# Unit 0's k through the SP queue in fp32, cast by VectorE and ScalarE, with k^T made ahead of q^T

**Chip, cores, metric.** One core of one Trainium2 chip. The metric is device time in microseconds (us) of one execution; lower is better. A run is one execution; an execution with a profile also leaves a trace.

## The reference

Two stages. Squared-ReLU attention over q, k, v of shape (8, 12, 448, 64) gives x of shape (3584, 768); two matrix products with a squared ReLU between them follow. Inputs and output are fp32.

```python
scores = scale * np.matmul(q, k.transpose(0, 1, 3, 2))
attn = np.maximum(scores, 0.0) ** 2 / S
x = np.matmul(attn, v)           # heads side by side: (3584, 768)
h = x @ w_in                     # (3584, 2048)
r = np.maximum(h, 0.0)
out = (r * r) @ w_out
```

## The kernel before

The kernel works in fp16 and fixes its own order of instructions. Attention is cut into 24 units of four heads. A unit's q and k come in as `[128, 2, 448]` tiles; for the first units TensorE transposes them by matmuls with an identity matrix that GpSimd makes (seven blocks, two halves each), and the blocks are copied out of PSUM to `qT` and `kT`. A score tile needs **one block of kT and all of qT**. Only unit 0 is exposed: nothing can hide its loads.

```python
def load16(n):
    tq = q16_p.tile([P, 2, J * D], FP16, name="q16", tag="q16")
    tk = q16_p.tile([P, 2, J * D], FP16, name="k16", tag="k16")
    nc.gpsimd.dma_start(out=tq, in_=heads(q, n))     # casts fp32 to fp16 on the way
    nc.gpsimd.dma_start(out=tk, in_=heads(k, n))
    q16s[n] = (tq, tk)

load16(0)
... # make_identity(nc, ident) on GpSimd; zeros on VectorE; a first ACTIVATE
load16(1); load_v(0); load16(2); load_v(1); load_v(2)

def turn_first(ps):
    ts = new_qkt()                                    # qT, kT
    for i, src in enumerate(q16s.pop(0)):             # q first, then k
        tps = slot(FP16)[:, i, 0:J * P].rearrange("p (j c) -> p j c", j=J)
        for j in range(J):
            for hh in range(2):
                nc.tensor.transpose(tps[64 * hh:64 * hh + 64, j],
                                    src[:, hh, j * D:(j + 1) * D], ident)
        if i:
            nc.scalar.activation(out=ts[i][:, 0], in_=tps[:, 0], func=AF.Copy)
        nc.vector.tensor_copy(ts[i][:, i:J], tps[:, i:J])
        warm(ps, 1)                                   # a matmul on zeros
    qkt[0] = ts

...
warm(ps, 10)
turn_first(ps)
s(0, 1); s(1); s(2); ...                              # scores, each evicted by ScalarE
```

A `slot` is a PSUM tile of two banks; the pool behind it holds two.

Of the kernel before, what the change touches and what calls it, by code (L numbers as in the profile page):

```python
# [11 lines left out]
FP16 = mybir.dt.float16  # L12
FP32 = mybir.dt.float32
AF = mybir.ActivationFunctionType
# [4 lines left out]
def kernel(  # L19
# [9 lines left out]
    nc = tc.nc  # L29

    B, H, S, D = q.shape
# [11 lines left out]
    P = 128  # L43
    J = 7
# [22 lines left out]
    g_p = ctx.enter_context(tc.tile_pool(name="gp", bufs=1))  # L67
    early = ExitStack()
    q16_p = early.enter_context(tc.tile_pool(name="q16p", bufs=3))

    PSUM = bass.MemoryType.PSUM
    s_p = ctx.enter_context(tc.tile_pool(name="sps", bufs=2, space=PSUM))
# [8 lines left out]
    def heads(t, n):  # L81
        b, u = divmod(n, NU)
        return t[b].rearrange(
            "(hh u hp) (p j) d -> u (hp p) hh (j d)", hh=2, hp=2, j=J)[u]
# [6 lines left out]
    def load16(n):  # L91
        tq = q16_p.tile([P, 2, J * D], FP16, name="q16", tag="q16")
        tk = q16_p.tile([P, 2, J * D], FP16, name="k16", tag="k16")
        nc.gpsimd.dma_start(out=tq, in_=heads(q, n))
        nc.gpsimd.dma_start(out=tk, in_=heads(k, n))
        q16s[n] = (tq, tk)

    def load_v(n):
        t = v_p.tile([P, 2, J * D], FP16, name="vt", tag="vt")
        nc.gpsimd.dma_start(out=t, in_=heads(v, n))  # L100
        vts[n] = t
# [12 lines left out]
    def new_qkt():  # L114
        return [qkt_p.tile([P, J, P], FP16, name=nm, tag=nm) for nm in ("qT", "kT")]
# [30 lines left out]
    def sums_w2(i):  # L146
# [4 lines left out]
        dst, x, y = ((t1, b12, b11), (t3, b22, b12), (t2, b22, t1), (nt4, b21, t2))[op]  # L151
        nc.vector.tensor_sub(dst[:, c], x[:, c], y[:, c])

    load16(0)
    ident = const_p.tile([P, P], FP16, name="ident", tag="ident")
    make_identity(nc, ident)
    zeros = const_p.tile([P, S], FP16, name="zeros", tag="zeros")
    nc.vector.memset(zeros, 0.0)
    junk = const_p.tile([P, 1], FP16, name="junk", tag="junk")
    nc.scalar.activation(out=junk, in_=zeros[:, 0:1], func=AF.Relu)  # L160
    load16(1)
    load_v(0)
    load16(2)
    load_v(1)
    load_v(2)
# [28 lines left out]
    def slot(dtype, third=False):  # L194
        return (third_p if third else s_p).tile(
            [P, 2, 2048 // mybir.dt.size(dtype)], dtype, name="slot", tag="slot")

    def warm(ps, n):
        for _ in range(n):
            nc.tensor.matmul(ps[:, 0, 0:S], lhsT=zeros[:, 0:P], rhs=zeros,  # L200
                             start=True, stop=True)

    def turn_first(ps):

        ts = new_qkt()
        for i, src in enumerate(q16s.pop(0)):
            tps = slot(FP16)[:, i, 0:J * P].rearrange("p (j c) -> p j c", j=J)
            for j in range(J):
                for hh in range(2):
                    nc.tensor.transpose(  # L210
                        tps[64 * hh:64 * hh + 64, j],
                        src[:, hh, j * D:(j + 1) * D], ident)
            if i:
                nc.scalar.activation(out=ts[i][:, 0], in_=tps[:, 0], func=AF.Copy)
            nc.vector.tensor_copy(ts[i][:, i:J], tps[:, i:J])
            warm(ps, 1)
        qkt[0] = ts

    def pe_transpose(n):
# [557 lines left out]
    ps = slot(FP32, True)  # L777
    warm(ps, 10)
    turn_first(ps)

    def s(t, times=2):
# [76 lines left out]
        name="mma", bufs=2, space=PSUM, reuse_waits="tile")))  # L858
# [5 lines left out]
    def some(part):  # L864
# [11 lines left out]
        name="mmb", bufs=2, space=PSUM, side="right", reuse_waits="tile")))  # L876
# [35 lines left out]
    for pr in range(1, B // 2):  # L912
# [3 lines left out]
        for i in range(21):  # L916
            ts = [t0 + 2 * i, t0 + 2 * i + 1]
# [86 lines left out]
```

## Time and profile before

| | before |
|---|---|
| median of 4 runs | 370.81 us (370.6 to 370.95) |
| span of the profiled run | 368.9 us |
| TensorE busy | 97% of the span |
| q landed after its issue at 1.27 us | 3.9 us |
| first score starts | 7.29 us |
| first eviction of a score by ScalarE starts | 7.72 us |

The span is the profiled execution from first to last instruction, and is about 1.8 us under the time. The lines are shown in the prediction, with a sentence on how to read each. Two habits help. In the chain of waits every piece was released by the one above it, so the sum from the top to "ACT at L266" is the length of the prologue. And the bracket at the end of a timeline line tells how long the engine idled before and which instruction or DMA ended that.

### The profile page before, as it was taken

The page shows a single profiled execution, that of the slowest core. Times are in us where ns is not written, and L with a number is a line of the kernel's source. Part 1 is how long each engine was busy: PE and PEld are TensorE (multiplying, and loading weights), DVE is VectorE, ACT ScalarE, POOL GpSimd, SP SyncE. Part 2 cuts the span into 40 slices and gives each one's busy share as a digit, 9 for nine tenths or more (in the row PEclk, how much of TensorE's full clock was granted, in tenths as well). Part 3 has the DMA queues.
Part 4 walks back from the last instruction along what each step waited for, and adds up shares of the span by engine and source line. Part 5 has one row for each costly group of instructions (what it writes and reads, how often), then busy time and mean ns, then how long its engine had stood idle before and what let it go on. Part 6 is the DMA issues. An engine that isn't in the chain of part 4 may idle for free.

```text
span 368.9 us, 8720 instructions
## 1 busy us (share of the span) xinstructions
PE 359.6 (97%) x3588; PEld 230.3 (62%) x3588; DVE 265.4 (72%) x470; ACT 247.5 (67%) x371; POOL 107.1 (29%) x128
## 2 busy tenths in 40 slices
PE   8899999999999999999999999999999999999994
PEld 3644445445555778875555588786555689976663
DVE  2997677997777787788585766989766686884442
ACT  3988894787676989876556588886765885532220
POOL 8545521846553155531225045140000000000001
PEclk9999999999999999999999999999999999999999
DMA  8999999999999999967699899692323300003333
GB/s 115 191 207 203 205 204 162 161 158 165 190 166 127 184 101 98 115 93 62 140 166 105 159 155 86 88 116 37 65 71 88 85 3 2 2 0 85 87 92 81
DMA packets 121159, 42.64 MB, mean 116 GB/s; under 512 B 100832, under 2 KB 117760, under 8 KB 121120
## 3 DMA queue, kind: packets, MB, share of 16 engines
q0 software_dynamic: 82912, 23.01, 62.3%
q1 hardware_dynamic: 38048, 18.98, 25.7%
q8 instruction: 28, 0.46, 0.5%
q10 hardware_dynamic: 160, 0.10, 0.1%
q14 instruction: 11, 0.09, 0.1%
HBM read 45.61 MB, written 11.01 MB: 153 GB/s over the span
## 4 chain that ended last, share of the span: by engine, by line
PE 90%; ACT 3%; DVE 3%; issue 2%; DMA 1%; POOL 0%; POOLq 0%; ACTq 0%
PE mm L725 34%; PE mm L538 27%; PE slot L262 10%; PE mm L409 9%; PE slot L317 7%; ACT at L266 3%; DMA k<-in_k_dram 1%; DVE at L297 1%; PE avt L280 1%; PE slot L238 1%; PE mm L238 0%; DVE at L369 0%; DVE xt L292 0%; ACT u L627 0%; DVE osb L632 0%
## 5 line engine op out<-in xcount | busy, mean ns | idle before, releaser
L266 ACT ACTIVATE at<-slot 128x896 f16<-128x896 f32 x168 | 145.8, 925 | 22.2 <-PE slot L262 22.2
L369 DVE TENSOR_TENSOR at<-at 128x896 f16<-128x896 f16 x147 | 87.1, 617 | 9.7 <-ACT at L266 9.6
L109 POOL DMA_DIRECT2D qs<-in_q_dram x36 | 35.3, 983 | 113.7 <-DMA qT<-qs 106.2
L725 PEld LDWEIGHTS <-s 128*128 128x128 f16 x440 | 41.5, 98 | 32.7 <-issue 3.6
L262 PE MATMUL slot<-qT,kT 64*64 64x448 f16 x744 | 56.8, 361 | 1.9 <-ACT at L266 1.4
L538 PEld LDWEIGHTS <-w 128*128 128x128 f16 x576 | 54.3, 98 | 5.1 <-issue 4.3
L538 PE MATMUL mm<-xt,w 128*128 128x224 f16 x432 | 48.9, 259 | 0.0
L725 PEld LDWEIGHTS <-g 128*128 128x128 f16 x336 | 31.7, 98 | 24.1 <-issue 4.7
L538 PEld LDWEIGHTS <-ws 128*128 128x128 f16 x432 | 40.3, 98 | 4.7 <-issue 4.7
L632 DVE SCALAR_TENSOR_TENSOR osb<-mm,u 128x384 f32<-128x384 f32 (+1 forms) x30 | 16.2, 542 | 36.4 <-ACT u L627 24.0
L725 PE MATMUL mm<-b,g 128*128 128x384 f16 x224 | 40.7, 326 | 0.0
L725 PE MATMUL mm<-b,s 128*128 128x384 f16 x216 | 39.6, 326 | 0.2 <-DVE s L594 0.2
L409 PE MATMUL mm<-xt,w 128*128 128x448 f16 x192 | 39.8, 354 | 0.0
L725 PE MATMUL mm<-t,s 128*128 128x384 f16 x224 | 39.3, 326 | 0.0
L109 POOL DMA_DIRECT2D ks<-in_k_dram x36 | 35.1, 976 | 9.4 <-DMA b<-in_moe_w_out_dram 5.8
L262 PEld LDWEIGHTS <-kT 64*64 64x64 f16 x744 | 19.0, 104 | 28.7 <-issue 23.3
L561 POOL DMA_DIRECT2D out_dram<-osb x2 | 1.1, 563 | 119.6 <-DVE osb L632 119.6
L627 ACT ACTIVATE u<-mm 128x384 f32<-128x384 f32 x28 | 13.8, 492 | 31.6 <-PE mm L725 27.1
L538 PE MATMUL mm<-x,ws 128*128 128x224 f16 x288 | 34.1, 259 | 0.0
L481 DVE CUSTOM_DVE_ANT_0 g<-mm,m 128x448 f16<-128x448 f32 x36 | 22.4, 622 | 15.1 <-PE mm L538 7.3
L317 PE MATMUL slot<-at,vt 64*64 64x448 f16 x588 | 31.9, 350 | 0.2 <-DVE at L369 0.2
L409 PEld LDWEIGHTS <-w 128*128 128x128 f16 x192 | 17.1, 98 | 19.2 <-issue 5.1
(76 smaller groups left out, 399.7 us busy)
## 6 DMA issues: line engine op xcount, KB each, us to landing
out_dram<-osb SPq DMA_DIRECT2D x52, 192.0 KB, 3.0
vt<-in_v_dram POOLq DMA_DIRECT2D x24, 224.0 KB, 6.2
qs<-in_q_dram POOLq DMA_DIRECT2D x36, 112.0 KB, 4.6
ks<-in_k_dram POOLq DMA_DIRECT2D x36, 112.0 KB, 5.0
w<-in_moe_w_in_dram POOLq DMA_DIRECT2D x8, 384.0 KB, 11.9
b<-in_moe_w_out_dram POOLq DMA_DIRECT2D x4, 768.0 KB, 17.1
q<-in_q_dram POOLq DMA_DIRECT2D x6, 224.0 KB, 7.9
k<-in_k_dram POOLq DMA_DIRECT2D x6, 224.0 KB, 8.3
```

What stands on the lines that cost most here:

```text
L109: nc.gpsimd.dma_start(out=t[:, :, hh, :], in_=heads(src, n)[:, hh].rearrange("p (j d) -> p j d", d=D))
L238: nc.tensor.transpose(pss[i][64 * hh:64 * hh + 64, i if n < 4 else 0, j * P:(j + 1) * P], src[:, hh, j * D:(j + 1) * D], ident)
L262: nc.tensor.matmul(ps[c, hh, 0:S], lhsT=kT[r, j, c], rhs=qT[r, :, c], start=True, stop=True)
L266: nc.scalar.activation(out=at, in_=ps[:, :, 0:S], func=AF.Relu, scale=SK)
L317: nc.tensor.matmul(ps[64 * hh:64 * hh + 64, hp, 0:S], lhsT=vt[r, hh, j * D:(j + 1) * D], rhs=at[r, hh, :], start=(j == 0), stop=(j == J - 1))
L369: lambda: nc.vector.tensor_mul(at, at, at), 0))
L409: nc.tensor.matmul(cell[0][:, 0:S], lhsT=w1[f // 4][:, m, (f % 4) * P:(f % 4 + 1) * P], rhs=xts[b][:, m, :], start=(m == 0), stop=(m == NM ...
L481: nc.vector._custom_dve(TENSOR_ADD_SAT, out=gs(s, hi, right), in0=acc(s, y), in1=keep[s, nm], s0=3.4e38, s1=0.0)
L538: nc.tensor.matmul(XY[s][y][:, r * Q:(r + 1) * Q], lhsT=left(k, i0 + 2 * s + r, m), rhs=right(k, m), start=(fresh and r == 0 and m == 0), ...
L627: nc.scalar.activation(out=t, in_=X[0][:, 0:HALF], func=AF.Copy, scale=CO)
L632: nc.vector.scalar_tensor_tensor(out=osb[row][:, c], in0=acc[0][:, 0:cc.stop - cc.start], scalar=CO, in1=keep[nm][:, cc], op0=ALU.mult, op ...
L725: nc.tensor.matmul(acc[0][:, 0:HALF], lhsT=left()[:, f], rhs=right[:, f], start=(fresh and f == 0), stop=(f == KH - 1), skip_group_check=n ...
```

## The change

Its intent: k of unit 0 doesn't queue behind q. SP starts it earlier, in fp32 (that SP could not have cast it on the way is not shown by a run; in the kernel before every load that casts is in GpSimd's queue); two idle engines cast it; k^T is then ready before q lands, and q^T is copied by two engines at once.

```diff
+        if n == 0:
+            raw = raw_p.tile([P, 2, J * D], FP32, name="rk", tag="rk")
+            nc.sync.dma_start(out=raw, in_=heads(k, n))
         nc.gpsimd.dma_start(out=tq, in_=heads(q, n))
+        if n == 0:
+            return lambda: (nc.vector.tensor_copy(tk[:, 0], raw[:, 0]),
+                            nc.scalar.activation(out=tk[:, 1], in_=raw[:, 1], func=AF.Copy))
         nc.gpsimd.dma_start(out=tk, in_=heads(k, n))
 ... # the casts are issued after the first ACTIVATE
-        for i, src in enumerate(q16s.pop(0)):
+        for i in (1, 0):
 ... # the same transposes, into tps[i]
+            warm(ps, 1)
             if i:
-                nc.scalar.activation(out=ts[i][:, 0], in_=tps[:, 0], func=AF.Copy)
-            nc.vector.tensor_copy(ts[i][:, i:J], tps[:, i:J])
-            warm(ps, 1)
+                nc.scalar.activation(out=ts[1][:, 0], in_=tps[1][:, 0], func=AF.Copy)
+        nc.vector.tensor_copy(ts[0][:, 0:4], tps[0][:, 0:4])
+        nc.scalar.activation(out=ts[0][:, 4:J], in_=tps[0][:, 4:J], func=AF.Copy)
+        nc.vector.tensor_copy(ts[1][:, 1:J], tps[1][:, 1:J])
```

More of the change, by code (lines that the diff above doesn't have):

```diff
@@ L69 @@
     q16_p = early.enter_context(tc.tile_pool(name="q16p", bufs=3))
+    raw_p = early.enter_context(tc.tile_pool(name="rawp", bufs=1))
     PSUM = bass.MemoryType.PSUM
@@ L93, in load16 @@
         tk = q16_p.tile([P, 2, J * D], FP16, name="k16", tag="k16")
+        q16s[n] = (tq, tk)
+        if n == 0:
+            raw = raw_p.tile([P, 2, J * D], FP32, name="rk", tag="rk")
+            nc.sync.dma_start(out=raw, in_=heads(k, n))
         nc.gpsimd.dma_start(out=tq, in_=heads(q, n))
+        if n == 0:
+            return lambda: (nc.vector.tensor_copy(tk[:, 0], raw[:, 0]),
+                            nc.scalar.activation(out=tk[:, 1], in_=raw[:, 1], func=AF.Copy))
         nc.gpsimd.dma_start(out=tk, in_=heads(k, n))
-        q16s[n] = (tq, tk)
     def load_v(n):
@@ L152, in sums_w2 @@
         nc.vector.tensor_sub(dst[:, c], x[:, c], y[:, c])
-    load16(0)
+    cast_k0 = load16(0)
     ident = const_p.tile([P, P], FP16, name="ident", tag="ident")
@@ L160 @@
     nc.scalar.activation(out=junk, in_=zeros[:, 0:1], func=AF.Relu)
+    cast_k0()
     load16(1)
@@ L205, in turn_first @@
         ts = new_qkt()
-        for i, src in enumerate(q16s.pop(0)):
-            tps = slot(FP16)[:, i, 0:J * P].rearrange("p (j c) -> p j c", j=J)
+        tps = {}
+        for i in (1, 0):
+            src = q16s[0][i]
+            tps[i] = slot(FP16)[:, i, 0:J * P].rearrange("p (j c) -> p j c", j=J)
             for j in range(J):
@@ L210, in turn_first @@
                     nc.tensor.transpose(
-                        tps[64 * hh:64 * hh + 64, j],
+                        tps[i][64 * hh:64 * hh + 64, j],
                         src[:, hh, j * D:(j + 1) * D], ident)
+            warm(ps, 1)
             if i:
-                nc.scalar.activation(out=ts[i][:, 0], in_=tps[:, 0], func=AF.Copy)
-            nc.vector.tensor_copy(ts[i][:, i:J], tps[:, i:J])
-            warm(ps, 1)
+                nc.scalar.activation(out=ts[1][:, 0], in_=tps[1][:, 0], func=AF.Copy)
+        nc.vector.tensor_copy(ts[0][:, 0:4], tps[0][:, 0:4])
+        nc.scalar.activation(out=ts[0][:, 4:J], in_=tps[0][:, 4:J], func=AF.Copy)
+        nc.vector.tensor_copy(ts[1][:, 1:J], tps[1][:, 1:J])
+        del q16s[0]
         qkt[0] = ts
```

## The prediction

> **What bounds the kernel now.** I read the page first (who is busy over the whole span), then the chain of waits over the first 60 us, then the timeline of the first 8 us, then the list of waits with a DMA as releaser. From the page:
>
> ```profile
> PE 359.6 (97%) x3588; PEld 230.3 (62%) x3588; DVE 265.4 (72%) x470; ACT 247.5 (67%) x371; POOL 107.1 (29%) x128
> ...
> PE 90%; ACT 3%; DVE 3%; issue 2%; DMA 1%; POOL 0%; POOLq 0%; ACTq 0%
> ```
>
> TensorE carries the kernel, and 90% of the chain that ended last is TensorE. DMA holds 1% of it, one piece: the load of k that this change touches. No gain can be larger than that piece and its neighbours. The chain of waits, first pieces (start, length, what):
>
> ```profile
> 2.12 4.17 DMA k<-in_k_dram
> 6.29 0.04 issue
> 6.33 0.60 PE slot L210 x14
> 6.94 0.02 issue
> 6.96 0.29 ACT kT L214
> 7.25 0.04 issue
> 7.29 0.41 PE slot L262 x4
> 7.70 0.02 issue
> 7.72 3.35 ACT at L266 x4
> ```
>
> This is the prologue: k lands at 6.29, is transposed, its first block is copied by ScalarE, the first score runs at 7.29, and at 7.72 the first ScalarE eviction of a score begins. From there evictions follow back to back (timeline: 6.58 us for 8, 0.82 us each), so the figure that the change must move is **7.72**. If the first eviction starts d earlier, the engine-bound chain after it starts d earlier. The timeline of the same stretch (start, length, engine, line):
>
> ```profile
> 1.16 3.92 PE L200 MATMUL slot<-zeros 128*128 128x448 f16 x10 [1.16 <-DVE zeros L158]
> 1.27 0.85 POOL L94 DMA_DIRECT2D q<-in_q_dram  x1 [0.83 <-POOLq L988]
> ...
> 2.12 0.75 POOL L95 DMA_DIRECT2D k<-in_k_dram  x1
> ...
> 5.21 0.52 PEld L210 LDWEIGHTS <-q 128*64 128x64 f16 x14 [0.93 <-DMA q<-in_q_dram]
> ...
> 5.94 0.62 DVE L215 COPY qT<-slot 128x896 f16<-128x896 f16 x1 [4.84 <-PE slot L210]
> ...
> 6.96 0.28 ACT L214 ACTIVATE kT<-slot 128x128 f16<-128x128 f16 x1 [4.72 <-PE slot L210]
> ...
> 7.27 0.56 DVE L215 COPY kT<-slot 128x768 f16<-128x768 f16 x1 [0.70 <-ACT kT L214]
> ```
>
> Three things are to be seen. q's transposes already wait for q (5.21) and k's come 1.1 us later. The ten warm-up matmuls fill TensorE until about 4.9: weight loads come every 0.373 us, the last matmul starts near 4.5. And the VectorE copy of k^T did not run beside ScalarE's copy of the same tile: the list says that it waited for it (7.24, then 7.27). Two engines that write parts of one tile are serialised here.
>
> The list of waits shows that after k no compute engine waits for an input load. All other DMA releases before the end are of the queues themselves, such as
>
> ```profile
> PEld L210 <- DMA q<-in_q_dram: 0.9, 1, 0.9
> POOL w L135 <- DMA q<-in_q_dram: 0.8, 2, 0.4
> PEld L210 <- DMA k<-in_k_dram: 0.4, 1, 0.4
> ```
>
> so earlier loads by themselves buy nothing beyond the first score.
>
> [...]
>
> **The change part by part.**
>
> 1. *k by SP.* It removes one POOL issue (0.75 us) and 4.17 us from issue to landing. SP is free at 0.7 us. Its stores of 192 KB land 2.1 us (least) to 2.8 us (median) after issue. k in fp32 is 448 KB; the loads stream some 200 GB/s as fp16 written, which is 400 GB/s as fp32 read, so 448 KB take about 1.15 us, against 0.5 us for 192 KB. Estimate: landing at 0.75 + 2.1..2.8 + 0.65 = 3.5..4.2 us.
>
> 2. *The casts.* [...]ScalarE half 0.54 us (the 128x448 row), side by side: k in fp16 is ready at 4.1..4.8. The table load ends at 2.03, so both engines are idle then.
>
> 3. *k's transposes first.* They start when the warm-ups end, S = 4.88, if the cast is in time; that is 1.45 us earlier than 6.33. At the warm clock the 14 weight loads take 0.51 us. If the clock rises near 5.4, as the slow first loads at 5.21 hint, nine of them run at 0.055 and five at 0.036: 0.70. Then one warm-up, 0.19, then q's transposes, 0.60 to their end (the chain's figure). q landed at about 5.2 before, so it isn't what they wait for. All transposes are done at 4.88 + 0.51..0.70 + 0.19 + 0.60 = 6.18..6.37, against 6.94 before: 0.57 to 0.76 us earlier. This is the gain.
>
> 4. *What follows the last transpose.* Before: ScalarE's one block of k^T, 0.29. After: all of q^T is needed by every score. The diff splits its copy, VectorE four blocks and ScalarE three, as if in parallel. The built program says otherwise: ScalarE's q^T copy waits for the third tick of VectorE's semaphore, and the ticks are memset, cast and VectorE's q^T copy. So they run one after the other, as the two k^T copies do in the trace. VectorE for 512 elements: 0.556 at 768 and 0.62 at 896 are 0.5 ns per element, so 0.43. ScalarE for 384: 278 ns + 256 x 0.825 ns = 0.49. With 0.03 between them the copies take 0.95 in place of 0.29: **0.65 us given back**. VectorE's k^T copy (0.56) runs beside ScalarE's part and is done about when the first score is, so it adds nothing.
>
> 5. *Sum.* -0.57..-0.76 + 0.65 = from 0.10 faster to 0.08 slower: first score at 7.2..7.4 (7.29 before), first eviction at 7.6..7.8 (7.72 before). After that nothing changes. POOL's later loads start some 0.7 us earlier, with k's bytes out of their queue, and nobody waited for those. The total stays: about **370.9 us**.
>
> **The rivals.**
>
> - *The copies overlap after all* (the intent of the diff). Then the first score comes 0.49 + 0.06 after the transposes, at 6.75..6.95, and the kernel gains 0.35 to 0.55 us: 370.4 to 370.6. For it: the diff is written so. Against it: the semaphore in the built program, and the same pair of engines serialised at 7.24 to 7.27.
> - *k comes late.* If SP's first load lands at 5 us instead of 4, because 256 rows of 1792 bytes are slower than my stores suggest or because it collides with q's load, then cast and transposes start near 5.6, and the first eviction at 8.4: 0.5 to 0.7 us slower, 371.5. For it: no plain load by SP is in this trace. Against it: the DMA engines show no work before 2.6 us.
> - *q comes late.* k's fp32 writes share the engines with q from 2.6 us on. q may be 0.4 us later than before (5.2) without harm, since it is not asked for before 5.6; and q no longer shares with k's other load. I give this little weight.
> - *Later loads matter.* v of unit 0 landed near 11.3 (a POOL issue that waited for it went at 11.31) and its first matmul starts at 11.50, so compute moved earlier by over 0.2 us could run into it. But POOL's queue is shorter by one load of 1.15 us, so it moves more than compute does.
>
> **Range and chances.** All outcomes lie within 1 us of 371, while 2% is 7.4 us. The spread of the three runs before is 0.35 us. Middle 370.9; low end 370.3 (copies overlap, or an early clock), high end 371.4 (k late). Faster by over 2%: 0.004. Slower by over 2%: 0.006. Within 2%: 0.99.
>
> **What the profile after should show.** Right if: k's transposes start near 4.9 with no idle TensorE between the tenth warm-up and them (step 3); [...]ScalarE's 128x384 q^T copy begins just as VectorE's 128x512 copy ends, with VectorE named as its releaser (step 4); first score within 0.15 us of 7.29; the rest of the trace shifted by that same amount. Step 1 is wrong if k's transposes name a cast or a DMA as releaser well after 5; step 4 is wrong if the two q^T copies overlap. The prediction as a whole fails if the time moves by over 0.6 us, above all if it does so with the first eviction still near 7.7: then something after the prologue depends on the loads, which I say it doesn't.

Cut from it are a paragraph of rules and figures that no trace of this case shows, and the two places that rested on them: VectorE's time for its half of the cast, and the mark that the casts end before 4.9. That time was not a term of the sum, which stands as recorded: -0.57 to -0.76 plus 0.65 us, from 0.10 faster to 0.08 slower, about 370.9 us. k's readiness at 4.1 to 4.8 rests on SP's landing at 3.5 to 4.2 and ScalarE's 0.54 us alone; that VectorE's half is the shorter no trace had shown then. SP's landing is an estimate: the measured 2.1 to 2.8 us of its 192 KB stores, and 448 KB at twice the 200 GB/s at which the trace shows the loads written in fp16. The trace before shows where the other terms come from: ScalarE's copies took 278 ns for 128 elements, 543 for 448 and 912 for 896 (0.825 ns per element from the first to the last), and 54 matmuls of 448 columns took 10.32 us (0.19 for one warm-up). The 0.055 us of a slow weight load is an estimate: in that trace the first six of q's weight loads start within 0.22 us from 5.21, and the clock record is full from 5.47.

## The result

The changed kernel takes **371.31 us** (median of 4 runs, 370.98 to 371.63) against 370.81. The ratio is 1.0014, with a 95% interval of 0.9996 to 1.0031: the same within 2%, and not clearly apart from 1. A ratio here is the mean time of one kernel's fast runs over that of the other's of the same rounds, so it isn't quite the ratio of the medians. The span grew from 368.9 to 369.2 us. The profiled run of the changed kernel was the fastest of its four (370.98), so its trace shows less of the loss than the medians do.

The chain of waits of the changed kernel, first pieces (start, length, what):

```profile
1.28 4.73 DMA q<-in_q_dram
6.00 0.04 issue
6.05 0.60 PE slot L220 x14
6.65 0.02 issue
6.67 0.44 DVE qT L226
7.11 0.02 issue
7.13 0.50 ACT qT L227
7.63 0.04 issue
7.67 0.41 PE slot L275 x4
8.08 0.02 issue
8.10 3.35 ACT at L279 x4
```

k is gone from the chain, and q has taken its place. The last transposes end at 6.65 in place of 6.94, but two copies follow one another before the first score starts at 7.67 (7.29 before). The first eviction starts at 8.10: 0.38 us later. The timeline of the same stretch:

```profile
4.25 0.58 ACT L102 ACTIVATE k<-rk 128x448 f16<-128x448 f32 x1 [2.02 <-DMA rk<-in_k_dram]
4.25 0.39 DVE L101 CAST k<-rk 128x448 f16<-128x448 f32 x1 [3.15 <-DMA rk<-in_k_dram]
4.73 0.56 PEld L220 LDWEIGHTS <-k 128*64 128x64 f16 x14 [0.46 <-DVE k L101]
...
6.04 0.42 PEld L220 LDWEIGHTS <-q 128*64 128x64 f16 x14 [0.56 <-DMA q<-in_q_dram]
6.05 0.58 PE L220 MATMUL slot<-ident,q 128*64 128x128 f16 x14 [0.29 <-DMA q<-in_q_dram]
...
7.13 0.49 ACT L227 ACTIVATE qT<-slot 128x384 f16<-128x384 f16 x1 [1.35 <-DVE qT L226]
```

k's part works as meant: cast by 4.83, transposed from 4.73 on. q's transposes then **wait for q**, whose load got slower: the weight loads for 0.56 us, the matmuls, which still had the warm-up to run, for 0.29. The list of DMA issues in the first 1.4 us (what, queue, size, us from issue to landing), of the kernel before and then of the changed one:

```profile
q<-in_q_dram POOLq DMA_DIRECT2D x1, 224.0 KB, 3.9
```

```profile
rk<-in_k_dram SPq DMA_DIRECT2D x1, 448.0 KB, 3.5
q<-in_q_dram POOLq DMA_DIRECT2D x1, 224.0 KB, 4.7
```

So there are two questions: what did the serial copies cost, and why did q land 0.8 us later?

### The profile page after: what moved, and what is told of

Its sections match the earlier page's. It is cut to its first block, busy times and chain, and to the rows that moved or that the text cites. A ratio compares the mean times of both kernels' runs of the same rounds, so it can differ in the third digit from the quotient of the medians.

```text
span 369.2 us, 8724 instructions
## 1 busy us (share of the span) xinstructions
PE 359.2 (97%) x3588; PEld 230.5 (62%) x3588; DVE 265.5 (72%) x471; ACT 248.8 (67%) x373; POOL 105.6 (29%) x127
## 4 chain that ended last, share of the span: by engine, by line
PE 90%; ACT 3%; DVE 3%; issue 1%; DMA 1%; POOL 0%; POOLq 0%; ACTq 0%
PE mm L738 34%; PE mm L551 27%; PE slot L275 10%; PE mm L422 9%; PE slot L330 7%; ACT at L279 3%; DMA q<-in_q_dram 1%; DVE at L310 1%; PE avt L293 1%; PE slot L251 1%; PE mm L251 0%; DVE at L382 0%; DVE xt L305 0%; ACT u L640 0%; DVE osb L645 0%
```

## The experiments

Twelve kernels ran. Each is told by q's landing (us after its issue), the start of the first eviction, and the span of the profiled run, beside the time. "A" edits start from the changed kernel, "B" edits from the kernel before. Single runs have no interval, and every kernel, the one before too, was traced in one execution alone: a landing or a first eviction below is that of one execution.

**One copy of q^T (A).** VectorE copies all seven blocks.

```diff
-        nc.vector.tensor_copy(ts[0][:, 0:4], tps[0][:, 0:4])
-        nc.scalar.activation(out=ts[0][:, 4:J], in_=tps[0][:, 4:J], func=AF.Copy)
+        nc.vector.tensor_copy(ts[0], tps[0])
```

> The changed kernel with q^T copied whole by VectorE, in one instruction, in place of four blocks on VectorE and then three on ScalarE. Theory (the two copies of one slot run one after the other, 0.44 + 0.02 + 0.50 = 0.96 us by the chain of waits): one copy of 896 elements takes 0.62, so the first score starts 0.33 us earlier, at 7.33, and the first eviction at 7.77 in place of 8.10; the time falls by 0.3 us to about 371.0. Rival (the copies are not what the first score waits for, q's late landing alone is): no change, first eviction at 8.10.

Measured: 371.03 us against 370.85 (ratio 1.0002, 0.9987 to 1.0017). q landed 4.8 us after issue. From the last transpose (6.75) to the first score (7.54) 0.79 us passed, where the changed kernel needed 1.02 (6.65 to 7.67). First eviction 7.97. So one engine is 0.23 us faster than two in turn. The expected 0.33 was not reached: after the single copy 0.14 us pass until the score, against 0.04 in the changed kernel.

**Two slots (A).** The last three blocks of q are transposed first and into the free bank of k's slot, so ScalarE and VectorE read different slots.

```diff
-            for j in range(J):
+            for j in ((4, 5, 6, 0, 1, 2, 3) if i == 0 else range(J)):
 ... # blocks 4 to 6 of q go to tps[2], which is bank 0 of k's slot
-        nc.scalar.activation(out=ts[0][:, 4:J], in_=tps[0][:, 4:J], func=AF.Copy)
+        nc.scalar.activation(out=ts[0][:, 4:J], in_=tps[2][:, 4:J], func=AF.Copy)
```

> The changed kernel with the last three blocks of q transposed first and into the other slot, so that ScalarE's copy shares no slot with VectorE's. Theory (the serialisation comes from sharing the slot in PSUM that is read, not from the tile that is written): ScalarE's q^T copy starts near 6.4, before VectorE's at 6.67, which ends at 7.1; first score at 7.15, first eviction at 7.58, 0.5 us before the changed kernel and 0.14 before the kernel before; time about 370.8. Rival (writing one tile from two engines serialises, or the two reads of PSUM slow each other): the copies still follow each other or take over 0.6 us each, first eviction at 8.0 or later.

Timeline of this kernel:

```profile
6.24 0.49 ACT L231 ACTIVATE qT<-slot 128x384 f16<-128x384 f16 x1 [0.54 <-PE slot L224]
...
6.46 0.42 DVE L230 COPY qT<-slot 128x512 f16<-128x512 f16 x1 [1.89 <-PE slot L224]
```

The copies now overlap, both released by TensorE, each as long as before, although both write the same `qT` tile. What serialised them was the **slot that they read**, not the tile that they write. (The wait is a semaphore in the built program, as the prediction found; no run here shows whether the hardware would need it.) From the last transpose (6.44) to the first score (7.04) 0.60 us pass in place of 1.02, so taking the serialisation away gave 0.42. q landed 4.5 us after issue, and the first eviction came at 7.46, before that of the kernel before. The profiled run had a span of 368.6 us, the shortest of all. Yet the four times were 370.38, 371.25, 371.43 and 370.26 (ratio 1.0, 0.9981 to 1.002): no gain that holds over runs. The trace is of the 370.38 run, so its early first eviction stands for the two shorter executions at most; the spans of the other two, 369.5 and 369.7, are about 1 us longer.

**Extra load (B).** The kernel before, with SP's fp32 load into a tile that nobody reads.

```diff
+        if n == 0:
+            raw = raw_p.tile([P, 2, J * D], FP32, name="rk", tag="rk")
+            nc.sync.dma_start(out=raw, in_=heads(k, n))
```

> The kernel before with SP's fp32 load of k added into a tile that nobody reads. Theory (the fp32 load takes DMA time from q's load, which is why q landed at 6.0 and not 5.2): q's transposes start at 6.0, k's at 7.1 (1.1 us later as before), first eviction at 8.5 in place of 7.72, time up by 0.8 us. Rival (q is late in the changed kernel for the order of POOL's own loads, not for the fp32 load): q's transposes at 5.2, first eviction at 7.7.

Measured: 371.31 us, one run. DMA issues of this kernel:

```profile
rk<-in_k_dram SPq DMA_DIRECT2D x1, 448.0 KB, 3.5
q<-in_q_dram POOLq DMA_DIRECT2D x1, 224.0 KB, 4.0
```

q landed only 0.1 us later, k at 6.77 in place of 6.29, the first eviction at 8.21. So in this execution the loads beside the fp32 load came 0.1 to 0.5 us later, but by itself it did **not** make q 0.8 us late. My first explanation fell here.

**Half the load (A).** SP loads half of k, and both casts read that half; the result is wrong (relative error 0.21).

> The changed kernel with SP loading only half of k (224 KB in place of 448), both casts read that half, so the result is wrong on purpose. Theory (bytes of the fp32 load delay q): q lands near 5.6, so the first eviction is about 0.4 us earlier than 8.10, near 7.7; k lands near 3.7 in place of 4.25. Rival (the delay of q does not depend on the bytes): q stays at 6.0 and the first eviction at 8.10.

Measured: 370.74 us, one run. k's half landed 2.6 us after issue, q 4.3 after, first eviction 7.86. Halving the bytes gives back half of q's delay, as expected. It also moved k's casts 0.9 us earlier, so this run doesn't tell bytes from timing. Its chain of waits runs through TensorE (the ten warm-ups, 3.91 us, then the transposes) and not through q, so its first eviction doesn't measure q's landing.

**Late identity (A).** By then two differences from "extra load" were in view: GpSimd's identity work stood right behind q's issue, and a cast ran while q was in flight. Here the identity goes behind unit 1's q and k.

```diff
-    make_identity(nc, ident)
 ...
     load16(1)
+    make_identity(nc, ident)
     load_v(0)
```

> The changed kernel with the two GpSimd instructions that make the identity moved behind the issues of unit 1's q and k, so that they no longer stand right behind q's issue. Theory (new, after the first four runs: q lands late in the changed kernel mostly because removing k's issue leaves GpSimd's identity work right behind q's load, 0.6 us of it; the fp32 load costs q only 0.15 to 0.3): q lands near 5.4 in place of 6.0, q's transposes start when k's are done, near 5.6, first eviction near 7.65 in place of 8.10. Rival 1 (sharing of the DMA engines with the fp32 load, then with unit 1's loads): q at 6.0 or later, first eviction 8.1 or later, since unit 1's loads are issued 0.55 us earlier. Rival 2 (VectorE's cast holds up q): also no change.

Measured: 371.43 us against 370.74 (ratio 1.0014, 0.9999 to 1.0029). q landed 5.0 us after issue, first eviction 8.44. The theory is refuted, the other way round. Not all of the 8.44 is q's: k's 14 transposes took 0.96 us here, against 0.73 in the changed kernel, and the chain of waits runs through them. TensorE's clock record is full from 6.4 us in this trace and from 4.4 in the changed kernel's; up to there I call the clock low. On the low clock the kernel before starts its 448-column warm-ups 0.373 us apart; later it runs 54 matmuls of 448 columns in 10.32 us, 0.191 each.

**Identity between q and k (B).** The same question from the other side, without any fp32 load.

```diff
         nc.gpsimd.dma_start(out=tq, in_=heads(q, n))
+        if n == 0:
+            make_identity(nc, ident)
         nc.gpsimd.dma_start(out=tk, in_=heads(k, n))
```

> The kernel before with the identity made between the issues of q and k of unit 0, in place of behind both; no fp32 load. Theory (identity work behind a load delays that load's landing): q lands near 5.8 in place of 5.17, although nothing shares the DMA engines with it that did not before; k lands 0.5 us later or so, being issued 0.54 later. Rival (only the fp32 load delays q): q lands at 5.2 or, with k's load further behind, earlier.

Measured: 374.13 us, one run. q landed 3.9 us after issue, as before: refuted again. k, issued 0.54 us later than before, landed 1.5 us later, at 7.76. TensorE's matmuls idled 1.72 us for it, and what followed cost more than the shift. Busy time by window, of the kernel before and of this one (columns: window, length, busy time of PE, PEld, DVE, ACT, POOL, then the share of TensorE's clock that was granted, the DMA share and GB/s):

```profile
10.00:20.00 10.00, 9.16 (x189) 6.09 (x185) 9.37 (x19) 10.00 (x14) 5.30 (x8) 1.00 1.24 198
```

```profile
10.00:20.00 10.00, 9.62 (x168) 5.84 (x164) 7.11 (x13) 8.90 (x11) 4.94 (x8) 0.79 1.26 204
```

The granted clock is 0.79 in place of 1.00 from 10 to 20 us, and ScalarE, the bound there, falls to 8.90 us busy of 10. The first eviction came 2.2 us late, the span grew by 3.4. The 1.72 us without a matmul (6.08 to 7.80) were followed by k's transposes at the low clock (0.96 us for 14, against 0.58 for q's before the idle time) and a granted clock of 0.50 from 7.4 to 14 us. That the idle time brought the lower clock is read from this one trace, not tested.

**Two slots and late identity (A).** Both edits together.

> Both repairs together: the two slots and the late identity. Theory: the serial copy cost 0.5 us and the identity 0.5 us, and they add: q's transposes start near 5.6, first score near 6.8, first eviction near 7.2, 0.9 us before the changed kernel, 0.5 before the kernel before: time near 370.4. Rival (something else, for example k's transposes on TensorE, holds q's transposes at 5.8): first eviction at 7.46, as with two slots alone.

Measured: 371.18 us (ratio 1.0008, 0.9991 to 1.0025). q 4.9 us after issue, first eviction 8.35. The first eviction is 0.89 us later than with two slots alone: q landed 0.4 us later, and TensorE was at the low clock, up to 7.1 (k's 14 transposes took 0.96 us, against 0.71, and q's 0.92, against 0.58), so its chain of waits runs through TensorE and not through q. This run tells nothing of whether the two edits add.

**Roles swapped (A).** q of unit 0 comes by SP, k by GpSimd; q^T is made first, with the late identity; block 0 of k^T goes to the free bank of q's slot, to be copied while the rest of k is transposed.

```diff
-            nc.sync.dma_start(out=raw, in_=heads(k, n))
+            nc.sync.dma_start(out=raw, in_=heads(q, n))
 ... # casts write tq; GpSimd loads k; the order is q, k
+                        (tps[2] if i and j == 0 else tps[i])[64 * hh:64 * hh + 64, j],
```

> The roles swapped: q of unit 0 in fp32 by SP, k by GpSimd, q^T first, late identity, and the first block of k^T in q's slot, so that ScalarE copies it while the rest of k is transposed. Theory: all that follows the late load is then one block's copy of 0.28 us in place of 0.96; k lands near 5.4, but its first transposes wait for VectorE's q^T copy, to about 6.1; first score near 6.7 and first eviction near 7.1; time near 370.3. Rival (the late load is what counts, and the copies are hidden): as with both repairs, 7.2.

Measured: 371.1 us (ratio 1.0004, 0.9989 to 1.0019). k, now first in GpSimd's queue, landed 5.7 us after its issue, later than q in any run; first eviction 8.36. What follows the late load is short now (0.93 us from the start of its transposes at 6.99 to the first score at 7.92), but the load itself ate that.

**Cast on ScalarE alone (A).** One ACTIVATE casts both halves.

```diff
-            return lambda: (nc.vector.tensor_copy(tk[:, 0], raw[:, 0]),
-                            nc.scalar.activation(out=tk[:, 1], in_=raw[:, 1], func=AF.Copy))
+            return lambda: nc.scalar.activation(out=tk, in_=raw, func=AF.Copy)
```

> The changed kernel with both halves of the cast on ScalarE, in one instruction of about 0.93 us, and none on VectorE. In the six runs with VectorE's fp32 cast so far the first load of the GpSimd queue landed 4.3 to 5.7 us after its issue, in the three without it 3.9 to 4.0; in the changed kernel 15 of its 16 engines were done by 5.29 and one at 6.00. Theory[...]: q lands at 5.3 or so, 4.0 us after its issue; k in fp16 is ready at 5.2, q's transposes start near 6.0 behind k's, first eviction 7.9 to 8.0. Rival (the straggling engine has another cause, for example GpSimd's own loads issued behind q): q lands 4.5 us after its issue or later.

(The mechanism that the theory gave is cut, as no run shows it. What it put to the test is whether VectorE's cast makes q late.)

Measured: 371.4 us (ratio 1.001, 0.9996 to 1.0024). q landed 5.2 us after issue, first eviction 8.62. VectorE casts nothing here and q is as late as ever. (q isn't alone in the way: the one long cast, 0.95 us, and k's transposes at the low clock, up to 6.2, 0.96 us, keep TensorE from q until about its landing.)

**VectorE's cast alone (B).** "Extra load" plus VectorE's cast into a tile that nobody reads.

```diff
+    nc.vector.tensor_copy(extra[1], extra[0][:, 0])
```

> The kernel before with SP's fp32 load and VectorE's 128x448 cast of half of it into a tile that nobody reads. Without the cast q landed 4.0 us after its issue and k at 6.77. Theory (VectorE's cast): q 4.5 us or more after its issue, first eviction later than the 8.21 of the run without the cast. Rival (not the cast): 4.0 again, 8.2.

Measured: 371.14 us, one run. The cast ran from 4.24 to 4.64, in the middle of q's flight; q landed 4.0 us after issue, first eviction 8.14. q's own issue by GpSimd had ended at 2.12, and the GpSimd issue that overlapped the cast, unit 1's k at 4.11, took 0.72 us, as it did without the cast. Together with the run above, VectorE's cast is cleared as sole cause.

**Both by SP (A).** q, then k, in fp32 by SP; both cast in halves; q^T first.

```diff
+            for r, t in zip(raws, (q, k)):
+                nc.sync.dma_start(out=r, in_=heads(t, n))
```

> A candidate for a faster kernel: q and then k of unit 0 in fp32 by SP, both cast by VectorE and ScalarE in halves, q^T first, so that only one block of k^T (0.28 us) follows the last transpose and nothing of unit 0 is in GpSimd's queue. By the measured 3.5 us to landing of the first and some 1.1 us more for the second: k lands near 5.3, fp16 by 5.9, transposes to 6.5, first score 6.8, first eviction 7.2 in place of 7.72; time 370.3, 0.5 us under the kernel before. Rival (the engine-bound chain after the prologue takes the gain back, or unit 1's and v's loads, pushed back by 900 KB of fp32, come too late): time 370.8 or more with the first eviction at 7.2.

Measured: 370.58 us (5 runs, 370.55 to 370.93) against 370.82 (9 runs); ratio 0.999, 0.9976 to 1.0004. The two loads landed 3.6 and 4.2 us after issue, and no load of the prologue was late. The first eviction came at 7.68, not 7.2: q's transposes ran at the low clock, up to 6.1 (0.95 us in place of 0.58), and VectorE's second cast took 0.65 us, not 0.39. The lowest median of all, but its interval reaches past 1, so I don't call it faster. The traced run is the slowest of the five; the spans of three others are 368.8, so their first eviction was probably nearer 7.3 (an estimate: 368.8 less the 361.5 of this trace).

**Old queue restored (A).** One candidate was left: what stands behind q in GpSimd's queue. Here the old load of k is put back there, into a spare tile.

```diff
+            spare = raw_p.tile([P, 2, J * D], FP16, name="sp", tag="sp")
+            nc.gpsimd.dma_start(out=spare, in_=heads(k, n))
```

> The changed kernel with GpSimd's old load of k put back behind q's, into a tile that nobody reads, so that GpSimd's queue is exactly that of the kernel before, while k^T still comes from SP's load and the two casts. So far q landed 3.9 to 4.0 us after its issue in all four kernels in which unit 0's k follows it in GpSimd's queue (with or without the fp32 load, with or without VectorE's cast), and 4.3 to 5.2 in all seven in which unit 1's q follows it. Theory (what stands behind q in GpSimd's queue decides how late its slowest engine is): q lands 4.0 us after issue, at 5.3, its transposes start behind k's near 5.6, first eviction near 7.65 in place of 8.10, although one more load is moved; time about 370.8. Rival (the work of the changed prologue itself, ScalarE's cast or k's early transposes, slows q): q lands 4.5 us after issue or later, first eviction 8.0 or later.

DMA issues of this kernel:

```profile
rk<-in_k_dram SPq DMA_DIRECT2D x1, 448.0 KB, 3.4
q<-in_q_dram POOLq DMA_DIRECT2D x1, 224.0 KB, 5.4
```

Measured: 371.68 us (ratio 1.0045, 1.0012 to 1.0078), first eviction 8.78. One of the four runs took 373.95 and pulls the ratio up; the other three, 371.56 to 371.77, all lie above the 370.57 to 370.9 of the kernel before. It is the one kernel whose interval lies clear of 1. GpSimd's queue is now that of the kernel before, and q is later than ever. Refuted too.

**What the runs say together.** Span less first eviction is nearly the same number in nearly all traces:

| kernel | q (swapped: k) landed, us after issue | first eviction | span | difference |
|---|---|---|---|---|
| before | 3.9 | 7.72 | 368.9 | 361.2 |
| changed | 4.7 | 8.10 | 369.2 | 361.1 |
| two slots | 4.5 | 7.46 | 368.6 | 361.1 |
| half the load | 4.3 | 7.86 | 369.0 | 361.1 |
| extra load | 4.0 | 8.21 | 369.5 | 361.3 |
| cast on ScalarE alone | 5.2 | 8.62 | 369.7 | 361.1 |
| old queue restored | 5.4 | 8.78 | 370.0 | 361.2 |
| both by SP | no such load | 7.68 | 369.2 | 361.5 |
| identity between q and k | 3.9 | 9.94 | 372.3 | 362.4 |

All others lie between 361.1 and 361.3. Only the run whose clock fell, and a little the one with both loads on SP, have more. So in these traces, but for that one run, what comes after the first eviction is shifted as one piece, and a prologue edit is worth its shift of that eviction.

The first eviction isn't steady from one execution to the next. Runs of one kernel differ in span by as much as 1.2 us (two slots, 368.5 to 369.7), and if the rest is as rigid there as between kernels, that spread is the prologue's. One candidate for it shows in the traces: TensorE's clock reaches full at 4.4 us in the changed kernel and 5.5 in the kernel before, but at 6.1 with both loads on SP, 6.2 with the cast on ScalarE alone, 6.4 with the late identity and 7.1 with two slots and late identity (the traces' clock records), though all begin the same warm-ups at 1.16; 14 transposes took 0.92 to 0.96 us on the low clock and 0.58 on the full one.

About q's lateness this much is shown. In most traces it is not a slower load as a whole but **stragglers among its 16 parts**. In these traces each of these loads raises its semaphore 16 times, and I call each raise a part (two expectations call it an engine; the page states the DMA queues' time as a share of 16 engines). In the changed kernel's trace 15 of q's 16 increments had come by 5.29 us and the last at 6.00; with the roles swapped, 15 by 5.28 and the last at 6.95; with "extra load" all 16 by 5.30; in the kernel before all by 5.17, the last under 0.1 us after the fifteenth. With the late identity seven of the 16 came late, from 5.50 to 6.29. The packet records of the swapped kernel have one packet of GpSimd's queue, started at 4.29, that took 1.73 us, where the median packet takes 0.09; that it belongs to this load is likely, but the record doesn't name the load. Later loads straggle too: unit 1's q in the kernel before had 15 parts by 7.74 and the last at 8.09. (The first packet came 1.10 us after the start of SP's issuing instruction, 0.74 to 1.84 in the changed kernel, and 1.56 us after that of GpSimd's, 1.27 to 2.83 in the kernel before; from the end of these instructions, 1.20 and 2.13, it is 0.64 and 0.70.) And in one trace of each kernel it goes with the whole changed prologue: all nine kernels that cast and transpose SP's load while the first load of GpSimd's queue is in flight landed that load 4.3 to 5.7 us after issue, all four that don't landed it in 3.9 to 4.0. The fp32 load, VectorE's cast, the place of the identity and the queue behind q are each cleared as sole cause. What the nine share and the four lack is ScalarE's cast into the unit's fp16 tile and, before q lands, TensorE's transposes of it and what follows them. I had no run that takes one of these alone, and no second trace of one kernel that would tell how much the landing varies by itself, so the cause **stays open**.

## Why the prediction was right, and where it was not

The time fell inside the range (370.3 to 371.4), near its upper end: 371.31 against 370.9. That it did is partly luck: the upper end was set for a late k, and k was on time; q was late. Two of its finer marks failed: the first score came at 7.67, not within 0.15 us of 7.29, and the first eviction at 8.10, not 7.6 to 7.8. By its steps:

- **Step 1, k by SP:** right. Landing at 4.2 us, at the upper edge of 3.5 to 4.2.
- **Step 2, the casts:** right. ScalarE's half took 0.58 us against 0.54, VectorE's 0.39; k was ready at 4.83 (4.1 to 4.8).
- **Step 3, transposes:** right for k, wrong for q. k's started at 4.73, a little before the 4.88 that I had worked out. q's should have started near 5.6; they started at 6.05. The sentence that failed is "q landed at about 5.2 before, so it isn't what they wait for", and with it the rival that I gave little weight: q had 0.4 us of slack by the prediction's sum and came 0.8 us later. The last transpose ended 0.29 us earlier than before, not 0.57 to 0.76. (Nine loads at 0.055 and five at 0.036 are 0.68, not 0.70, which changes nothing.)
- **Step 4, the serial copies:** right in mechanism and size. Last transpose to first score took 1.02 us against 0.35, so 0.67 given back (0.65 predicted). ScalarE names VectorE's copy as its releaser, and the two-slot run removed 0.42 of it by removing the shared slot. The reason given beside the first profile, that two engines write parts of one tile, was wrong: it is the slot that both read.
- **Step 5, the sum:** -0.29 + 0.67 = 0.38 us later, where I had 0.10 earlier to 0.08 later. The mis-sized term is the gain of step 3.
- **Nothing after the prologue depends on it:** right for this change; the difference in the table is 361.2 before and 361.1 after. (v of unit 0 landed at 11.0 in the kernel before, not near 11.3: that is when the issue behind it went.)
- The rival that q shares the DMA engines with k's fp32 writes had the right victim and mostly the wrong reason: with the fp32 load alone beside it q landed 4.0 us after issue against 3.9 ("extra load").

In short, the change takes k out of the chain, exposes q, slows q, and lengthens what follows q. The author's gain, 0.35 to 0.55 us by the first rival's working, went into the serial copy (0.42 of it recoverable) and q's stragglers (0.29 by the matmuls' wait, 0.45 against the predicted start near 5.6).

## What to carry to other kernels

When a load is moved off the path, look up what becomes last in its stead and how much slack that has, in a run of the new kernel: the new last load had about 0.4 us, and its landing moved by 0.8. Two engines that copy parts of one PSUM tile may run in turn (here the second copy began at 7.13, as the first ended at 7.11; from two slots they overlapped, from 6.24 and 6.46); look at the releaser of the second copy, and give each its own tile. A prologue edit is read from one number, here the start of the first eviction: it says where the time of that execution went. But it varies from execution to execution as the time does, so a difference of some 0.1 us between two kernels with one trace each is not yet an effect of the edit: trace each kernel more than once.
